# Fused attention and two feed-forward layers: heads, loads and gate sums of the opening rearranged

## The chip, the cores and the metric

One core of a Trainium2 chip runs the whole program. TensorE (PE) multiplies matrices, VectorE (DVE), ScalarE (ACT) and GpSimd (POOL) work on elements, SyncE (SP) issues most transfers, and ACT's queue can issue some. The metric is the device time of one execution in microseconds (us), as the median of several runs.

## What is computed

The reference, cut to its core: causal attention with a decay by the cumulative sum of logged gates, over 4 x 8 heads of 576 rows and 64 columns, and then two feed-forward layers on 2304 rows.

```python
scores = scale * np.matmul(q, k.transpose(0, 1, 3, 2))        # 4 x 8 heads, 576 x 64
cum = np.cumsum(np.log(np.clip(f, 0.0001, 1.0)), axis=-1)
decay = cum[:, :, :, None] - cum[:, :, None, :]
scores = np.where(causal, -1000000000.0, scores + decay)
attn = softmax(scores)
x = (attn @ v), laid out as 2304 x 512
h = x @ w_in;  x = np.maximum(0.01 * h, h) @ w_out            # 512 -> 2048 -> 512
h = x @ w_in2; out = (h * sigmoid(h)) @ w_out2
```

The term `cum[:, :, :, None]` is the same for all keys of a row, and a softmax over the keys does not change by it.

## The kernel before

**Tiling.** Each sequence of 576 rows is cut into a first half of 256 rows (two blocks of queries) and a second of 320 (three). A unit of work is a head of one half: heads 0 to 7 are the eight heads of the first half of sequence 0, heads 8 to 15 those of its second half, and so on to 63. The rows that attention gives go to tiles named ring, in two parts (a rounded one and the rest). When the first 256 rows are complete (all of heads 0 to 7), `hidden` starts: products named hps of ring tiles with weights w, in steps of two weights of 128 columns; `summed` adds their outcome into acc. The words of the weights are loaded (`first_weights`, issued in `fetch`), and converted by ACT and DVE into two parts (`conv_in`, `conv_out`: one ACT step at L1478, DVE steps at L1479, L1480 and L1482, a rounding by ACT and a difference by DVE at L307).

**A head.** `score` issues for each block of queries a product (sps) and, on DVE, a minimum with the mask (L668), then on ACT an exponential (L711); the sums of the shares, their reciprocal (`shares`) and the scaling (L719 on DVE or L721 on ACT) follow. `transp` transposes the shares on PE (tps, L770), they are copied to pf, and `weigh_pair` multiplies two heads with their values (av, L840) and writes the ring. `attention` (L918) sets the order: the product of head n, then a wait for the transposes ("tail") of head n-1, then the transposes of head n are started and the product of head n+1 follows.

**Gates.** `gates` loads fs (L405 for 512 rows, L403 for the last 64), has it clamped (`clamp`, L331, by GpSimd), takes logs on ACT, loads the table for the exponential ("warm", L417) and sums along the rows by products with a triangle, cps (L429). Heads 0 and 1 (`n < DIRECT`) add the gates in their own product from fs and the triangle (L681). The other heads have two more rows under the 64 of q and k: beside the queries the negated sum and ones, beside the keys ones and the sum. For heads 2 to 7 `first_rows` copies them from cps into cfr (L485 on DVE, L486 on ACT) and SP moves them into the tiles of q and k (L143 in the profile, two transfers for each pair of heads). From head 8 on they come from memory: `plain_rows` writes cum_p (three rows), `split_rows` writes cum_d (six rows, split into a rounded part and the rest), and each head loads its rows from these.

**Order.** A planner (`Plan`) runs at build time: every step is a generator that asks for an engine with a cost and a rank, the lowest rank that is ready goes first, and what the planner picks is the order in which each engine's instructions stand in the program. Its costs set the order alone and no time on the chip. Where PE has nothing ready before the first hps, it gets a filler, a product into fps that nothing reads (`fillers`, L392 and L395); fillers end when the planner has issued the first step of hps. Conversions of weights have rank 1, the work of heads rank 0. Word loads wait for cf (the gate rows of `first_rows` made), those from the third on for "rows" (these rows landed). SP issues one transfer after the other; a wait ahead of it holds all behind it.

Of the kernel before, what the change touches and what calls it, by code (L numbers as in the profile page):

```python
# [19 lines left out]
STG_BUFS = 3  # L20
# [14 lines left out]
DIRECT = 2  # L35
EARLY = 2
FAVOR = 0.3
LAT = 0.11
PE_LAT = 0.4
# [29 lines left out]
class Plan:  # L69
# [8 lines left out]
    def __init__(self):  # L78
        self.now, self.count = 0.0, 0
        self.events, self.ready, self.free = [], {}, {}  # L80
        self.seen, self.waiting = {}, {}
        self.taken, self.given, self.queue = {}, {}, {}
        self.dma_free = 0.0
        self.filler = {}
# [46 lines left out]
    def issue(self, eng):  # L131
# [11 lines left out]
        fn()  # L143
        end = self.free[eng] = self.now + cost
# [95 lines left out]
def fused_kernel(ctx, tc, qt, kt, va, vb, ft, w1, wi2, wo2, out):  # L240
# [26 lines left out]
    cum_d = dram.tile([H * B, 6, S], F32, name="cum_d")  # L267
    cum_p = dram.tile([H * B, 3, S], F32, name="cum_p")
# [44 lines left out]
    def build_consts():  # L313
# [14 lines left out]
        def clamp(k):  # L328
            n, sl = opened["parts"][k]
            yield wait(("fs", k))  # L330
            yield op("pool", 0.35, lambda: nc.gpsimd.tensor_scalar(  # L331
# [5 lines left out]
        def fills():  # L337
# [9 lines left out]
            for r in range(2):  # L347
                yield zero(0.25, cum_rows[0][r][:, 1 - r], 1.0)
            signal("ones")

        def selects():
# [6 lines left out]
            yield from clamp(0)  # L358
            yield from clamp(1)
# [11 lines left out]
        yield par(fills(), selects())  # L371

    cum_rows = {}

    def gates(cp):
# [5 lines left out]
        cp3 = cp.tile([H * B, 3, S], F32, name="cp3")  # L381
        cr = cp.tile([H * B, 6, S], F32R, name="cr")
        warm = cp.tile([1, 1], F32, name="warm")
        z = cp.tile([128, 256], F32R, name="z")
        opened.update(tri=tri, fs=fs, parts=parts, ones=(cp3[:, 1, :], f32(cr[:, 2:4, :])))
# [14 lines left out]
        def logs(k):  # L400
            n, sl = parts[k]
            if k:
                yield dma(8e3, lambda: nc.sync.dma_start(out=fs[0:n, nfull, :], in_=ft[nfull * 128:S, :]), -1)  # L403
            else:
# [12 lines left out]
                    op("act", 1.4, lambda: nc.scalar.activation(warm, fs[0:1, 0, 0:1], ACTF.Exp), 0)))  # L417
        pss = []
        banks = []
        for i, (t0, tn) in enumerate(HALF):  # L420
# [12 lines left out]
            for piece in ([todo] if i == 0 else [[c] for c in todo]):  # L433
                yield op("pe", sum(pe_cost(tn - 128 * c + t0, 4) for c in piece),
                         lambda: [sums(c) for c in piece], 1 if i else -1)
            pss.append(ps)
            if i == 0:
                cf = cum_rows[0]
                p.start(first_rows(ps, cf))
        signal("cum")  # L440

        def plain_rows():
            yield wait("rows_set")
            for i, ((t0, tn), ps) in enumerate(zip(HALF, pss)):
                w = slice(t0, t0 + tn)
                if i == 0:
                    yield act(tn, lambda: nc.scalar.copy(cp3[:, 2, w], ps), 0)
                    yield wait(("cf", 0), ("cf", 1))
                else:
                    yield dve(tn, lambda: nc.vector.tensor_scalar(  # L450
                        cp3[:, 2, w], ps, cp3[:, 2, t0 - 1:t0], None, op0=ALU.add), 0)
                give(("av", "sp")[i], banks[i])
                yield dve(tn, lambda: nc.vector.tensor_scalar(
                    cp3[:, 0, w], cp3[:, 2, w], -1.0, None, op0=ALU.mult), 0, True)
            yield dma(221e3, lambda: nc.sync.dma_start(out=cum_p, in_=cp3), 0)
            signal("cum_p")

        def split_rows():
            c, hi, lo = cp3[:, 0], cr[:, 0], cr[:, 1]
            yield act(S, lambda: nc.scalar.copy(hi, c))  # L460
            yield dve(S, lambda: nc.vector.tensor_tensor(lo, c, f32(hi), op=ALU.subtract))
            for dst, src in ((cr[:, 4], hi), (cr[:, 5], lo)):
                yield act(S, lambda: nc.scalar.mul(dst, f32(src), -1.0))
            yield dma(442e3, lambda: nc.sync.dma_start(out=cum_d, in_=f32(cr)))
# [7 lines left out]
    def first_rows(ps, cf):  # L472

        def rows(r, step):
            yield wait("ones")
            yield step
            signal(("cf", r))
            yield par(*[seq(
                dma(8e3, partial(nc.sync.dma_start, out=first[i][64 + r:65 + r], in_=cf[r][2 * i:2 * i + 2]), i - H),
                signals(("row", r, i)),  # L480
            ) for i in range(DIRECT // 2, H // 2)])
            give("stg", cum_rows[1][r])

        yield par(
            rows(0, dve(256, lambda: nc.vector.tensor_scalar(cf[0][:, 0], ps[0:H], -1.0, None, op0=ALU.mult), 0)),  # L485
            rows(1, act(256, lambda: nc.scalar.copy(cf[1][:, 1], ps[0:H]), 0)),  # L486
        )
# [31 lines left out]
    def load_first():  # L519
# [3 lines left out]
        def group(i):  # L523

            t = first[i] = slot(i, [66, 2, 2, tn], F32, "qk0")
            def move(r, src):
                dst, src_ = t[0:64, :, r], src[0, 2 * i:2 * i + 2, 0:64, 0:tn].rearrange("h d s -> d h s")
                if i == 0 and r:
                    yield op("act", 0.6, lambda: nc.scalar.dma_start(out=dst, in_=src_), 0, 2.0)
                else:  # L530
                    yield dma(131e3, lambda: nc.sync.dma_start(out=dst, in_=src_), 0 if i else -2)

            if i > 1:
                yield wait(("cf", 0), ("cf", 1))
            yield par(move(0, qt), move(1, kt))
            if 2 * i >= DIRECT:
                yield wait(("row", 0, i), ("row", 1, i))
# [18 lines left out]
    def load_head(n):  # L556
# [30 lines left out]
        if plain(n):  # L587
            k2 = hd.tile([66, ke], F32, tag="m1", name="k2")
            s1 = hd.tile([66, tn], F32, tag="s1", name="s1")
            heads[n].update(s1=s1, m1=k2)  # L590
            if e == 0:
# [4 lines left out]
                seq(wait("cum_p"), dma(4e3, lambda: nc.sync.dma_start(out=k2[64:66], in_=cum_p[g, 1:3, 0:ke]), 0)),  # L596
                seq(wait("cum_p"), dma(4e3, lambda: nc.sync.dma_start(out=s1[64:66], in_=cum_p[g, 0:2, t0:ke]), 0)),
# [7 lines left out]
        m2 = hd.tile([68, ke], F32R, tag="m2", name="m2")  # L605
        s1 = hd.tile([128, tn], F32R, tag="s1", name="s1")
        s2 = hd.tile([68, tn], F32R, tag="s2", name="s2")
# [15 lines left out]
        def rows():  # L623
            yield wait("cum_d")
            yield dma(4e3, lambda: nc.sync.dma_start(out=f32(s2[64:68]), in_=cum_d[g, 0:4, t0:ke]), 0)
            yield dma(4e3, lambda: nc.sync.dma_start(out=f32(m2[64:68]), in_=cum_d[g, 2:6, 0:ke]), 0)
# [9 lines left out]
    def loads():  # L636
# [5 lines left out]
        yield wait(("cf", 0), ("cf", 1))  # L642
# [1139 lines left out]
```

## Time and profile before

| what | us |
|---|---|
| median of 3 runs (994.35 to 1001.07) | 994.56 |
| profiled execution, time | 996.5 |
| its span, first to last instruction | 994.7 |
| PE busy in the span | 988.4 |
| DVE busy | 770.7 |
| ACT busy | 637.3 |

The mean granted clock of PE is 0.999 of full. A busy PE is not PE at its peak: matmuls are pipelined and their ends are modelled, and the fillers count as busy. The opening is the first 48 us, in which the first eight heads run, the first weights are converted and PE gets fillers.

### The profile page before, as it was taken

How to read it: one execution, taken by the hardware profiler on the slowest of the kernel's cores; microseconds unless marked ns; L12 is line 12 of the kernel's file. 1: busy time of each engine (PE TensorE's matmuls, PEld its weight loads, DVE VectorE, ACT ScalarE, POOL GpSimd, SP SyncE). 2: the span in 40 equal slices, each digit the busy share in tenths (PEclk: the TensorE clock that was granted, in tenths of full speed). 3: DMA queues.
4: the chain of work that ended last, by engine and by line, in shares of the span. 5: the costliest groups of instructions: out<-in, count | busy, mean ns of one | idle time of the engine just before them, and what ended most of it. 6: DMA issues, size and time to landing. Idle time of an engine off the chain costs nothing.

```text
span 994.7 us, 21101 instructions
## 1 busy us (share of the span) xinstructions
PE 988.4 (99%) x7911; PEld 951.3 (96%) x7911; DVE 770.7 (77%) x1843; ACT 637.3 (64%) x1389; POOL 107.9 (11%) x137
## 2 busy tenths in 40 slices
PE   9999999999999999999999999999999999999998
PEld 7777779999999999999999999999999999999998
DVE  6998968878888787887767799566762389988884
ACT  6866567667787777887664667565654576444442
POOL 2000003122222222342111010000000000000000
PEclk9999999999999999999999999999999999999999
DMA  6943433221242222332302686568985586445442
GB/s 202 309 127 118 146 112 108 65 85 42 74 128 72 85 60 60 93 114 82 105 29 101 222 302 219 186 227 287 333 299 198 164 281 191 149 134 163 128 128 64
DMA packets 98238, 148.99 MB, mean 150 GB/s; under 512 B 8324, under 2 KB 69404, under 8 KB 96056
## 3 DMA queue, kind: packets, MB, share of 16 engines
q1 hardware_dynamic: 97992, 147.51, 46.0%
q8 instruction: 62, 1.02, 0.4%
q14 instruction: 40, 0.33, 0.1%
q10 hardware_dynamic: 144, 0.13, 0.1%
HBM read 99.21 MB, written 43.66 MB: 144 GB/s over the span
## 4 chain that ended last, share of the span: by engine, by line
PE 95%; DMA 3%; SPq 1%; DVE 0%; ACT 0%; issue 0%; DVEq 0%
PE hps L970 21%; PE acc L1049 19%; PE m L1264 18%; PE m L1435 18%; PE sps L688 6%; PE tps L770 5%; PE av L881 4%; PE acc L1043 2%; PE av L840 1%; DMA wsd<-in_w_dram 1%; DMA wsg<-in_w_dram 1%; DMA s<-cum_p 1%; DMA wsr<-in_w_dram 1%; PE fps L392 0%; SPq L1520 0%
## 5 line engine op out<-in xcount | busy, mean ns | idle before, releaser
L970 PE MATMUL hps<-ring,w 128*128 128x256 f32 x1728 | 259.3, 287 | 0.0
L970 PEld LDWEIGHTS hps<-ring,w 128*128 128x128 f32 x1728 | 228.5, 191 | 4.5 <-issue 2.9
L1049 PE MATMUL acc<-g,dec 128*128 128x256 f32 x1344 | 199.3, 285 | 0.0
L1264 PE MATMUL m<-xc,w 128*128 128x256 f32 x1536 | 185.4, 282 | 0.0
L1264 PEld LDWEIGHTS m<-xc,w 128*128 128x128 f32 x1536 | 184.3, 191 | 0.0
L1435 PE MATMUL m<-w,gc 128*128 128x256 f32 x1512 | 182.3, 283 | 0.0
L1435 PEld LDWEIGHTS m<-w,gc 128*128 128x128 f32 x1512 | 181.6, 191 | 0.6
L1049 PEld LDWEIGHTS acc<-g,dec 128*128 128x128 f32 x1344 | 177.3, 191 | 0.5
L299 ACT CAST gc<-g 128x512 fp32r<-128x512 f32 (+1 forms) x144 | 79.0, 567 | 82.8 <-DVE g L1097 35.6
L711 ACT ACTIVATE sc<-sc,st 128x576 f32<-128x576 f32 (+4 forms) x160 | 93.0, 582 | 51.8 <-DVE st L668 50.8
L299 ACT CAST dec<-wo 128x512 fp32r<-128x512 f32 x112 | 69.5, 620 | 46.4 <-PE acc L1049 46.0
L307 DVE TENSOR_TENSOR gc<-g,gc 128x512 fp32r<-128x512 f32 (+1 forms) x144 | 87.2, 620 | 8.2 <-ACT gc L299 6.9
L668 DVE CUSTOM_DVE_ANT_0 sc<-sps,zmask 128x288 f32<-128x288 f32 (+4 forms) x160 | 72.1, 452 | 17.8 <-PE sps L688 12.0
L307 DVE TENSOR_TENSOR dec<-wo,dec 128x512 fp32r<-128x512 f32 x89 | 62.9, 707 | 25.1 <-ACT dec L299 24.6
L770 PE MATMUL tps<-ident,sc 66*107 66x66 f32 (+3 forms) x480 | 66.6, 268 | 0.5 <-DVE sc L719 0.4
L788 DVE TENSOR_TENSOR pl<-tps,pt 107x320 fp32r<-107x320 f32 (+2 forms) x114 | 54.4, 509 | 14.9 <-ACT pt L787 14.3
L1097 DVE TENSOR_TENSOR g<-g 128x256 f32<-128x256 f32 x144 | 58.8, 420 | 8.4 <-DMA g<-g_d 7.5
L688 PE MATMUL sps<-m,s 68*128 68x288 f32 (+9 forms) x264 | 59.9, 308 | 0.0
L770 PEld LDWEIGHTS tps<-ident,sc 66*107 66x107 f32 (+3 forms) x480 | 54.4, 151 | 4.3 <-issue 1.8
L787 ACT CAST pt<-tps 107x320 fp32r<-107x320 f32 (+2 forms) x114 | 45.9, 447 | 16.8 <-PE tps L770 16.3
L307 DVE TENSOR_TENSOR g<-hps,g 128x512 fp32r<-128x512 f32 x65 | 44.6, 686 | 15.6 <-ACT g L299 14.8
L1000 ACT ACTIVATE hps<-hps 128x512 f32<-128x512 f32 x65 | 37.9, 583 | 23.0 <-PE hps L970 22.2
(140 smaller groups left out, 1389.5 us busy)
## 6 DMA issues: line engine op xcount, KB each, us to landing
g_d<-z SPq DMA_DIRECT2D x16, 1024.0 KB
g<-g_d SPq DMA_DIRECT2D x32, 512.0 KB
w_d<-f SPq DMA_DIRECT2D x16, 896.0 KB
ws<-w_d SPq DMA_DIRECT2D x56, 256.0 KB
wst<-in_wi_dram SPq DMA_DIRECT2D x16, 512.0 KB
wst<-in_wo_dram SPq DMA_DIRECT2D x16, 512.0 KB
qk<-in_kt_dram SPq DMA_DIRECT2D x24, 288.0 KB
wss<-in_w_dram SPq DMA_DIRECT2D x10, 512.0 KB
```

Of the source, the lines that this page charges most:

```text
L299: ("act", act_cost(n, base), lambda: nc.scalar.copy(dst, src), 0.0),
L307: ("dve", dve_cost(n), lambda: nc.vector.tensor_tensor(dst, a, b, op=ALU.subtract), 0.0),
L668: yield dve(w, lambda: nc.vector.tensor_tensor_reduce(out=sc[0:qn, k0:k0 + w], in0=ps[0:qn], in1=zmask[0:qn, z0:z0 + w], scale=-0.125, sca ...
L688: nc.tensor.matmul(ps[0:qn], ht[x][:, qs], ht[y][:, k0:k0 + w], start=r == 0, stop=r == len(ops) - 1)
L711: yield act(kn, lambda: nc.scalar.activation(sc[0:qn, 0:kn], sc[0:qn, 0:kn], ACTF.Exp, scale=-1.0, bias=st[0:qn, 2 * i + a:2 * i + a + 1], ...
L770: nc.tensor.transpose(ps[0:k1 - k0, o:o + qn], ht["p"][i][0:qn, k0:k1], ident[0:qn, 0:qn])
L788: yield op("dve", dve_cost(width), lambda: nc.vector.tensor_tensor(pts[1][0:kw], ps[0:kw], f32(pt[0:kw]), op=ALU.subtract), 0, PE_LAT)
L970: nc.tensor.matmul(hp_t[:, part], w[:, wi, c * 128:(c + 1) * 128], x[xi][:, c, :], start=(part == 0 and c == 0 and r == 0), stop=(c == KC ...
L1049: nc.tensor.matmul(o, w[:, wi, c * 128:(c + 1) * 128], g[:, gi, part * T:(part + 1) * T], start=(start and r == 0 and c % 2 == 0), stop=(s ...
L1097: ("dve", dve_cost(n), lambda: nc.vector.tensor_tensor(dst, a, b, op=op_), 0.0),
L1264: nc.tensor.matmul(dst[:, a], w[:, wi, c * 128:(c + 1) * 128], x[:, xi, c], start=start and a == 0 and c == 0 and r == 0, stop=stop and c ...
L1435: nc.tensor.matmul(banks[b][:, e], t[:, gi, a * 128:(a + 1) * 128], w[:, wi], start=begin and a == 0 and r == 0, stop=jp == NP // 2 - 1 an ...
```

## The change

Three heads are under way in place of two while the first eight run: the wait ahead of the next head is for the transposes of all heads up to n-2 (`AHEAD`). The loads of q and k for heads 4 to 7 no longer wait for the gate rows; their key loads, as that of heads 0 and 1 already, go by ACT's queue, those of heads 4 to 7 behind the load of the Exp table. Ranks of the first loads change. The clamp goes from GpSimd to DVE. The queries' gate row is dropped everywhere: products have 65 (or 64 + 66) rows, `first_rows` makes one row with ACT alone and moves three rows in place of six, cum_p has two rows and cum_d four, and the negations on DVE and ACT go. The sums cps of the first half get rank 0.5 in place of -1, the cum_p transfer -1 in place of 0. A transpose asks for its PSUM bank after its SBUF tiles. The planner starts its time at 0.85 us, doubles PE's costs ahead of 6.9 us and adds 0.13 us to every hand-over but SP's ahead of 45 us. No line of the diff changes how many word loads may be under way.

```diff
+AHEAD = 2
+OPEN = 0.85
+COLD = 6.9
+TIGHT = 45.0
+HOP = 0.13
-        self.now, self.count = 0.0, 0
+        self.now, self.count = OPEN, 0
         fn()
+        if eng == "pe" and self.now < COLD:
+            cost *= 2
+        if eng != "sp" and self.now < TIGHT:
+            lat = (LAT if lat is None else lat) + HOP
...
-    cum_d = dram.tile([H * B, 6, S], F32, name="cum_d")
-    cum_p = dram.tile([H * B, 3, S], F32, name="cum_p")
+    cum_d = dram.tile([H * B, 4, S], F32, name="cum_d")
+    cum_p = dram.tile([H * B, 2, S], F32, name="cum_p")
...
-            yield op("pool", 0.35, lambda: nc.gpsimd.tensor_scalar(
+            yield op("dve", 0.2, lambda: nc.vector.tensor_scalar(
                 fs[0:n, sl], fs[0:n, sl], 0.0001, 1.0, op0=ALU.max, op1=ALU.min), 0)
...
-                yield dma(8e3, lambda: nc.sync.dma_start(out=fs[0:n, nfull, :], in_=ft[nfull * 128:S, :]), -1)
+                yield dma(8e3, lambda: nc.sync.dma_start(out=fs[0:n, nfull, :], in_=ft[nfull * 128:S, :]), -2.5)
...
-                    op("act", 1.4, lambda: nc.scalar.activation(warm, fs[0:1, 0, 0:1], ACTF.Exp), 0)))
+                    op("act", 1.4, lambda: nc.scalar.activation(warm, fs[0:1, 0, 0:1], ACTF.Exp), -1), signals("warm")))
...
-                         lambda: [sums(c) for c in piece], 1 if i else -1)
+                         lambda: [sums(c) for c in piece], 1 if i else 0.5)
...
-                yield dve(tn, lambda: nc.vector.tensor_scalar(
-                    cp3[:, 0, w], cp3[:, 2, w], -1.0, None, op0=ALU.mult), 0, True)
-            yield dma(221e3, lambda: nc.sync.dma_start(out=cum_p, in_=cp3), 0)
+            yield dma(147e3, lambda: nc.sync.dma_start(out=cum_p, in_=cp3), -1)
...
-            for dst, src in ((cr[:, 4], hi), (cr[:, 5], lo)):
-                yield act(S, lambda: nc.scalar.mul(dst, f32(src), -1.0))
-            yield dma(442e3, lambda: nc.sync.dma_start(out=cum_d, in_=f32(cr)))
+            yield dma(295e3, lambda: nc.sync.dma_start(out=cum_d, in_=f32(cr)))
...
-        yield par(
-            rows(0, dve(256, lambda: nc.vector.tensor_scalar(cf[0][:, 0], ps[0:H], -1.0, None, op0=ALU.mult), 0)),
-            rows(1, act(256, lambda: nc.scalar.copy(cf[1][:, 1], ps[0:H]), 0)),
-        )
+        yield wait("ones")
+        yield act(256, lambda: nc.scalar.copy(cf[:, 1], ps[0:H]), 0)
+        signal("cf")
+        yield par(*[seq(
+            dma(8e3, partial(nc.sync.dma_start, out=first[i][64:65], in_=cf[2 * i:2 * i + 2]), i - H),
+            signals(("row", i)),
+        ) for i in range(DIRECT // 2, H // 2)])
...
-                if i == 0 and r:
-                    yield op("act", 0.6, lambda: nc.scalar.dma_start(out=dst, in_=src_), 0, 2.0)
+                if r and i != 1:
+                    if i:
+                        yield wait("warm")
+                    yield op("act", 0.6, lambda: nc.scalar.dma_start(out=dst, in_=src_), 0 if i else -2, 2.0)
                 else:
-                    yield dma(131e3, lambda: nc.sync.dma_start(out=dst, in_=src_), 0 if i else -2)
-
-            if i > 1:
-                yield wait(("cf", 0), ("cf", 1))
+                    yield dma(131e3, lambda: nc.sync.dma_start(out=dst, in_=src_), -2 if i else -2.6)
...
-            i_sp = yield take("sp", 3)
-            ps = ps_at.tile([128, width], F32, tag="sp", name="tps")
...
+        for w in work:
+            w[4] = yield take("sp", 3)
+            w[3] = ps_at.tile([128, w[2]], F32, tag="sp", name="tps")
...
-            if prev is not None:
-                yield wait(("tail", prev))
+            back = AHEAD if n < H - 1 else 1
+            yield wait(*[("tail", m) for m in range(max(0, n - H), n - back + 1)])
...
-        yield wait(("cf", 0), ("cf", 1), "v0_sent")
+        yield wait("cf", "v0_sent")
```

## Rows read from the trace of the kernel before

**Rows 1.** The page's first part: busy us, share of the span, instructions.

```profile
PE 988.4 (99%) x7911; PEld 951.3 (96%) x7911; DVE 770.7 (77%) x1843; ACT 637.3 (64%) x1389; POOL 107.9 (11%) x137
```

**Rows 2.** Tile fps: count, ns min/median/max of one, first and last start in us.

```profile
L395 PE MATMUL fps<-zmask x112: 272/275/377, 12.3 to 42.1; 128*128 128x128 f32 x112
L392 PE MATMUL fps<-z x15: 415/415/583, 1.3 to 4.4; 128*128 128x256 f32 x15
```

**Rows 3.** Stretches: length; busy PE, PEld, DVE, ACT, POOL; PE clock; DMA share; GB/s.

```profile
6.00:12.00 6.00, 6.00 (x26) 3.53 (x25) 2.35 (x12) 3.98 (x11) 2.05 (x5) 1.00 0.67 209
12.00:18.00 6.00, 6.00 (x49) 5.06 (x48) 5.31 (x24) 4.33 (x13) 0.00 (x0) 1.00 0.65 201
18.00:42.00 24.00, 24.00 (x178) 19.13 (x175) 22.05 (x73) 20.48 (x57) 0.00 (x0) 1.00 0.95 301
42.00:48.00 6.00, 5.48 (x41) 4.87 (x40) 4.85 (x14) 4.69 (x10) 0.00 (x0) 1.00 0.97 281
48.00:100.00 52.00, 51.95 (x321) 39.28 (x321) 47.26 (x122) 34.29 (x77) 0.00 (x0) 1.00 0.41 129
```

**Rows 4.** PE in order of time: start us, us, line, operation, names, count.

```profile
4.76 1.49 PE L429 MATMUL cps<-tri,fs 128*32 128x256 f32 x4
6.18 0.72 PE L679 MATMUL sps<-qk 64*128 64x128 f32 x2
...
12.93 0.49 PE L770 MATMUL tps<-ident,sc 128*128 128x128 f32 x3
...
25.63 2.84 PE L395 MATMUL fps<-zmask 128*128 128x128 f32 x24
...
33.59 0.49 PE L770 MATMUL tps<-ident,sc 128*128 128x128 f32 x3
...
39.64 0.96 PE L970 MATMUL hps<-ring,w 128*128 128x256 f32 x6
...
979.50 11.20 PE L1435 MATMUL m<-w,gc 128*128 128x256 f32 x92
```

**Rows 5.** DVE by line, 6 to 42 us: busy us, mean ns | idle before.

```profile
L668 DVE CUSTOM_DVE_ANT_0 sc<-sps,zmask 128x128 f32<-128x128 f32 (+4 forms) x21 | 8.3, 396 | 4.5 <-PE sps L681 3.6 <-PE sps L688 0.8
...
L307 DVE TENSOR_TENSOR w<-ct,w 128x512 fp32r<-128x512 f32 x4 | 2.7, 687 | 0.0
L1480 DVE SCALAR_TENSOR_TENSOR ct<-cy,ct 128x512 int32<-128x512 int32 x4 | 2.7, 684 | 0.0
L1482 DVE SCALAR_TENSOR_TENSOR ct<-wsr,ct 128x512 int32<-128x512 int32 x3 | 2.0, 678 | 0.0
...
L453 DVE TENSOR_SCALAR cp<-cp 32x256 f32<-32x256 f32 (+1 forms) x2 | 0.6, 284 | 0.0
...
L485 DVE TENSOR_SCALAR cfr<-cps 8x256 f32<-8x256 f32 x1 | 0.4, 413 | 3.7 <-PE cps L429 3.7
```

**Rows 6.** PE by line, 0 to 12.2 us: the products of heads 0 and 1.

```profile
L681 PE MATMUL sps<-tri,fs 128*128 128x128 f32 (+1 forms) x12 | 2.8, 343 | 0.0
L679 PE MATMUL sps<-qk 64*128 64x128 f32 (+1 forms) x8 | 2.6, 410 | 0.0
```

**Rows 7.** In order of time: the clamp, and the fourth weight's last step.

```profile
2.97 0.64 POOL L331 TENSOR_SCALAR fs<-fs 128x128 f32<-128x128 f32 x1 [0.53 <-DMA fs<-in_ft_dram]
...
40.40 0.69 DVE L307 TENSOR_TENSOR w<-ct,w 128x512 fp32r<-128x512 f32 x1
```

**Rows 8.** Issues of transfers in order of time, by ACT's and SP's queue.

```profile
0.81 0.71 ACTq L529 DMA_DIRECT2D qk<-in_kt_dram  x1
...
6.73 1.47 SPq L143 DMA_DIRECT2D qk<-cfr  x2
8.24 0.86 SPq L1520 DMA_DIRECT2D wsr<-in_w_dram  x2
...
11.58 0.67 SPq L531 DMA_DIRECT2D qk<-in_qt_dram  x1
...
19.20 0.42 SPq L1520 DMA_DIRECT2D wsr<-in_w_dram  x1
```

## What I predict, blind

> **What bounds the kernel now.** I read the page's first part first: TensorE (PE) is busy for 99% of the span [rows 1]. That number hides the opening, because the kernel itself keeps PE busy there with products that nothing reads. So the second view is that of one tile, fps, the target of these fillers: 15 of them before 4.4 us and 112 between 12.3 and 42.1 us [rows 2]. A run of 24 takes 2.84 us [rows 4], 0.118 us each, so the 112 cost 13.2 us; the first 15 cost 3.6 us. Behind 42.1 us there are none.
>
> The third view is the table of stretches [rows 3]. From 48 to 100 us PE is uncovered for 0.05 us, so from there on nothing is won by starting single pieces sooner: what the opening saves shifts the rest forward as a block. The same table says what paces the opening. VectorE (DVE) works 5.31 of 6 us and then 22.05 of 24 from 12 to 42 us, which is 27.36 of 30, or 91%; ScalarE (ACT) has 24.81 of 30. From 6 to 12 us DVE has only 2.35 of 6.
>
> The fourth view is the order of time on PE [rows 4]. The transposes of heads 0 and 7 start at 12.93 and 33.59 us, so the eight heads of the first block pass at 20.66/7 = 2.95 us each, and the first hidden product of the network (hps) starts at 39.64 us, 6.05 us behind the last of them. Fillers run until then. So the questions are by how much hps comes forward, and whether PE is fed from there.
>
> **The change, part by part.** *The first head.* Today the gate sums (cps) go ahead of head 0's product: they start at 4.76 us, and the product (sps) starts at 6.18 [rows 4]. DVE waits 3.7 us until cps ends, and then 3.6 us in all for the four products of heads 0 and 1 [rows 5]. With rank 0.5 in place of -1 the sums go behind products that are ready, so head 0 starts up to 6.18 - 4.76 = 1.42 us sooner. The clamp, 0.64 us on GpSimd [rows 7], moves to DVE, which waits then; the trace has no clamp by DVE. Its nearest tensor_scalar, two of 0.28 us at the mean [rows 5], would save 0.36 us; at the price of GpSimd it saves nothing. The bounds of both edits together are 0 and 1.42 + 0.36 = 1.8 us. Against the upper end stands that head 0 moves into the slow stretch: the first 15 products of 256 columns are 3.6/15 = 0.24 us apart [rows 2], those at the end 11.20/92 = 0.122 [rows 4], though the table shows a granted clock of 1.00, that is 2.4 GHz, throughout. For it stands that the third head also falls into the 3.65 us that DVE has idle from 6 to 12 us. I take 1.8.
>
> What the moved sums delay: the products of heads 0 and 1 keep PE 2.6 + 2.8 = 5.4 us [rows 6], 2.7 us a head, so the gate row cf comes up to 2.7 us later, and with it the rows of heads 2 to 7 and all word loads, which wait on cf. The first words go out at 8.24 us now [rows 8], then by 10.9. I cost this at nothing, because the heads' work on DVE covers it; without that cover it costs up to 2.7 us.
>
> *Work that is gone.* DVE loses the negated gate row, 0.41 us, and two negations of the plain rows, 0.57 us together [rows 5]: 0.98 us, all at the place where it sets the pace. I count 1.0; nothing if the holes stay empty. A fill of ones goes too, where DVE waits anyway: nothing. ACT loses two negations and gains two load issues of 0.71 us each [rows 8]; even without the loss, 1.42 us lie in the 5.2 that ACT has idle in those 30: nothing, and 1.42 without that cover. One row less in a product changes no column count: no PE time. cum_d and cum_p lose three rows of 32 x 576 values of 4 bytes, 0.22 MB; at 301 GB/s [rows 3] this is 0.7 us of transfer, hidden by DVE's pace, and worth 0.7 us where transfers bound.
>
> *Queues.* SP issues without a pause from 6.73 us on: gate rows at 1.47/2 = 0.74 us each, loads at 0.67; the third word goes at 19.20 [rows 8]. Three gate rows go, 2.2 us. The four loads of heads 4 to 7 leave this stretch, 4 x 0.67 = 2.7 us: two go to ACT behind its Exp table, two to an earlier place on SP. So SP gains 4.9 us and gives up to 2.7 back by the late cf; later words come 2.2 to 4.9 us sooner. The transfers are 0.65 to 0.67 busy from 6 to 18 us and 0.95 from 18 to 42 [rows 3], so there is room ahead of 18 us. Worth nothing by itself, but it lets the words keep step with a shift of some 4 us.
>
> A rule speaks against these edits: by the Trainium skill (DMA: Bandwidth & Descriptors, Issuing engines are not separate DMA queues) issuing from several engines saves only the issue time, which it calls small beside the transfer. The trace agrees only in part: an issue takes 0.67 to 0.74 us on a queue without a pause [rows 8]. By the rule the early loads would bring nothing, as in the second rival; by the rows they move words by 2.2 us or more.
>
> *The third head.* Now the product of head n+1 waits for the transposes of head n-1, then for those of n-2. This can only fill DVE's holes from 12 to 42 us, 2.64 us. I take half, 1.3; bounds 0 and 2.6. The later request for a bank in the transposes and the planner's hops of 0.13 us change the order alone, and no row shows them; beyond 48 us the nearest is the 0.05 us that PE loses, so I take nothing, with the 0.5 us that PE loses from 42 to 48 [rows 3] as the other bound, a loss or a gain.
>
> *Sum.* 1.8 + 1.0 + 1.3 = 4.1 us. The profiled execution has a span of 994.7 us and a time of 996.5, which is 1.9 above the runs' median of 994.56. So the span would be 990.6, the profiled time 992.4, and the median 990.4 us, which I predict.
>
> **The rivals.** *Heads quicker than DVE's share allows.* With three heads under way the eight may pass at DVE's and ACT's bare work, and the 6.05 us behind the last may shrink; hps would come 6.5 to 10 us sooner. For it: 13.2 us of fillers are there to take. Against it: DVE has 3.65 + 2.64 = 6.3 us idle from 6 to 42 us, and with the 0.98 that goes, 7.3 us is the most unless conversions are left for after hps. Time 984.6 to 988.
>
> *The transfers set the pace.* They are 0.95 to 0.97 busy from 18 to 48 us [rows 3]. If so, heads finish sooner and hps waits for weights; the 0.7 us of bytes and up to 1.4 of the earlier start are left: 992.5 to 993.9. Against it: DVE, at 91%, hardly waits on a load there.
>
> *Slower: heads starve the weights.* Heads have rank 0 on DVE and ACT, conversions rank 1. Three of a conversion's four DVE steps take 0.69 + 0.68 + 0.68 = 2.05 us [rows 5]. The second hidden step needs the fourth weight, ready now at 41.09 us [rows 7], 1.45 us behind the first hps. If the third head and late words push conversions back by two, PE meets a hole without fillers, which end with the first step: 4.1 us later weights, less the 1.45, 2.7 us lost, 997.3; with the words' 2.7 on top, 1000. It decides where the fourth weight is ready later than 42.5 us. For it: DVE's 91%. Against it: the work ahead of that weight is the same sum, less 0.98.
>
> *It does not do what it says.* The words are called unlimited, but nothing in the diff alters how many are loaded, and the key loads of heads 4 to 7 wait for the Exp table and are not at once. If heads keep today's pace for that, the first head's gain alone is left, at most 1.8 us: 992.7 to 994.5.
>
> **How the numbers follow.** Forecast, 988 to 992.5: 0.50. Transfers bound, 0.12, and no third head in effect, 0.08, both 992.5 to 994.6. Quicker heads, below 988: 0.17, of which 0.05 below 984.6. Slower than 994.6: 0.13, of which 0.03 above 1004.5, where more than the priced delays would have to meet. About 1% (9.9 us) is what a measurement of this kernel can tell from no change, so faster has 0.05, same 0.92, slower 0.03. The range leaves out the ends of the two outer cases, 985.5 to 997.0; the forecast's own is 988 to 992.5.
>
> **What the profile would show.** Right: head 0's sps near 4.8 us, transposes of heads 0 and 7 near 11 and 29.5, hps near 35.5; some 4 us fewer fillers, about 78 records; DVE at 95% or more from 12 to 36 us; PE still covered from 48 us on. Wrong: as many fillers as now; PE waiting for w or a load between 36 and 48 us; first words behind 11 us; a span that moves by another amount than hps.

## The result, and the profile after

The changed kernel takes 1004.48 us (median of 5 runs, 1002.41 to 1007.24), the kernel before 994.93 beside it (994.35 to 1001.07): a ratio of 1.0084, 95% interval 1.0057 to 1.0111. It is slower by 8 to 10 us: the interval lies above 1, though mostly within the 1% that the prediction took for no change. The time is outside the range of 985.5 to 997.0, and the forecast of 990.4 had the sign wrong. The profiled execution took 1007.24 us, with a span of 1005.5 against 994.7.

The page's first part of the changed kernel, to hold against [rows 1]:

```profile
PE 994.8 (99%) x7883; PEld 953.4 (95%) x7883; DVE 769.4 (77%) x1839; ACT 637.6 (63%) x1388; POOL 108.9 (11%) x136
```

PE's share is again 99%, and says as little as before. The stretches, against [rows 3]; columns as there:

```profile
6.00:12.00 6.00, 6.00 (x16) 2.84 (x14) 0.73 (x4) 1.86 (x7) 0.35 (x1) 1.00 0.81 224
12.00:18.00 6.00, 6.00 (x19) 3.73 (x19) 1.26 (x7) 1.74 (x6) 0.00 (x0) 1.00 0.61 176
18.00:42.00 24.00, 24.00 (x154) 18.45 (x152) 20.05 (x77) 17.48 (x51) 0.00 (x0) 1.00 0.83 268
```

From 12 to 18 us PE is covered throughout and yet gets through 19 products where it did 49, and DVE works 1.26 of 6 us instead of 5.31. The granted clock is shown as 1.00, but that is no reading of these stretches: the first record of the clock in this trace starts at 23.53 us (in the kernel before at 6.70), and ahead of it the view prints 1.00. PE in order of time, against [rows 4], says what happened:

```profile
4.75 0.79 PE L675 MATMUL sps<-qk 64*128 64x128 f32 x2
...
6.20 1.49 PE L436 MATMUL cps<-tri,fs 128*32 128x256 f32 x4
...
18.30 0.85 PE L767 MATMUL tps<-ident,sc 128*128 128x128 f32 x3
...
18.94 1.06 PE L684 MATMUL sps<-qk 65*128 65x256 f32 x2
...
20.64 1.49 PE L402 MATMUL fps<-zmask 128*128 128x128 f32 x6
...
25.03 0.60 PE L684 MATMUL sps<-qk 65*128 65x256 f32 x2
...
32.58 1.95 PE L402 MATMUL fps<-zmask 128*128 128x128 f32 x16
...
38.45 0.55 PE L767 MATMUL tps<-ident,sc 128*128 128x128 f32 x3
...
44.31 0.96 PE L965 MATMUL hps<-ring,w 128*128 128x256 f32 x6
```

The same two products take 1.06 us at 18.94 and 0.60 at 25.03. Until about 23.5 us every product goes at half the later pace; before, the pair of products at 6.18 us is the last that is slow. The transposes of head 0 come at 18.30 us instead of 12.93, and hps at 44.31 instead of 39.64. Here PE is the limit of the opening, which no step of the prediction had.

That is half of the loss. For the rest I laid both traces over each other by PE's own work: fillers left out, each product counted by its columns at full pace (957.9 us in all, the same in both), and the time read at which PE has done so much of it. Kernels of the experiments below stand beside it; a minus is a lead over the kernel before.

| work done, us | 25 | 90 | 100 | 200 | 300 | 400 | 600 | 800 | end |
|---|---|---|---|---|---|---|---|---|---|
| before, at us | 45.83 | 112.83 | 123.91 | 226.59 | 328.44 | 430.15 | 630.98 | 831.31 | 989.46 |
| changed | +4.90 | +4.54 | +5.79 | +5.02 | +7.11 | +9.05 | +10.83 | +10.72 | +10.76 |
| e1 | -0.17 | -0.78 | -0.62 | -1.13 | +0.95 | +2.88 | +4.69 | +4.53 | +4.44 |
| e4 | -4.53 | -3.47 | -4.23 | -4.82 | -2.71 | -0.76 | +1.05 | +2.22 | +3.32 |
| e5 | -2.24 | -1.88 | -1.88 | -1.92 | -1.91 | -1.90 | -1.90 | -0.99 | -0.04 |
| e6 | -4.25 | -3.68 | -3.68 | -3.71 | -3.70 | -3.71 | -3.72 | -3.20 | -2.39 |
| e7 | -0.38 | -1.30 | -1.30 | -1.32 | -0.38 | +0.54 | +1.29 | +2.87 | +2.60 |
| e13 | -1.48 | -1.04 | +0.21 | -0.55 | +1.51 | +3.48 | +5.33 | +5.02 | +4.74 |
| e10 | -0.47 | -0.46 | -0.46 | -0.46 | -0.45 | -0.45 | -0.45 | -0.52 | -0.58 |
| e14 | -4.47 | -3.77 | -3.77 | -3.79 | -3.79 | -3.76 | -3.78 | -3.14 | -2.67 |

The table compares single executions. That of the kernel before, at 996.5 us, lies 1.0 to 1.9 us above the medians of 994.56 to 995.49 that this kernel has in all, so by medians the leads are smaller by that; that of the changed kernel is the slowest of its five.

The changed kernel has lost 4.9 us by 50 us, loses 1.25 at about 123 us, gains 0.8 back by 230, and loses 5.8 between 230 and 642 us, where it computes the same as before. PE's waits from 200 to 640 us (total us, times, longest); the kernel before has none in this stretch:

```profile
PE hps L965 <- DVE g L317: 1.5, 1, 1.5
PE av L878 <- DVE xf L891: 0.5, 1, 0.5
PE tps L767 <- DVE sc L715: 0.4, 1, 0.4
PE sps L684 <- DVE pl L785: 0.2, 1, 0.2
PE av L878 <- DVE pl L785: 0.2, 1, 0.2
PE av L878 <- DVE ring L310: 0.2, 1, 0.2
```

Each is a short wait for a piece of DVE's work. Ahead of the longest, ACT and DVE each do a step of a weight w directly before theirs of the g that PE waits for; how much of the 1.5 us this costs, and what stands ahead in the other waits, isn't shown:

```profile
598.68 0.61 ACT L1677 CAST w<-ws 128x512 fp32r<-128x512 f32 x1
599.18 0.58 ACT L309 CAST g<-hps 128x512 fp32r<-128x512 f32 x1
...
599.32 0.69 DVE L317 TENSOR_TENSOR w<-ws,w 128x512 fp32r<-128x512 f32 x1 [0.21 <-ACT w L1677]
599.92 0.68 DVE L317 TENSOR_TENSOR g<-hps,g 128x512 fp32r<-128x512 f32 x1
...
600.75 0.95 PE L965 MATMUL hps<-ring,w 128*128 128x256 f32 x6 [1.48 <-DVE g L317]
```

The same view of waits from 48 to 200 us has one row, a word of the second weights:

```profile
PE acc L1038 <- DVE wo L1477: 2.0, 1, 2.0
```

### The profile page after: what moved, and what is told of

Read it like the earlier page. It is cut to its first block, busy times and chain, and to the rows that moved or that the text cites. A ratio compares the mean times of both kernels' runs of the same rounds, so it can differ in the third digit from the quotient of the medians.

```text
span 1005.5 us, 21027 instructions
## 1 busy us (share of the span) xinstructions
PE 994.8 (99%) x7883; PEld 953.4 (95%) x7883; DVE 769.4 (77%) x1839; ACT 637.6 (63%) x1388; POOL 108.9 (11%) x136
## 4 chain that ended last, share of the span: by engine, by line
PE 91%; DVE 4%; ACT 2%; DMA 1%; issue 1%; POOL 0%; DVEq 0%; POOLq 0%; ACTq 0%
PE hps L965 19%; PE m L1259 18%; PE acc L1044 17%; PE m L1430 15%; PE sps L684 6%; PE tps L767 5%; PE av L878 4%; PE acc L1038 2%; PE av L837 2%; PE fps L402 1%; DVE gc L317 1%; DMA g<-g_d 1%; DVE w L317 1%; DMA ws<-w_d 0%; PE sps L677 0%
## 5 line engine op out<-in xcount | busy, mean ns | idle before, releaser
L664 DVE CUSTOM_DVE_ANT_0 sc<-sps,zmask 128x288 f32<-128x288 f32 (+4 forms) x160 | 71.7, 449 | 23.5 <-PE sps L684 12.1
L317 DVE TENSOR_TENSOR dec<-wo,dec 128x512 fp32r<-128x512 f32 x86 | 60.1, 699 | 28.4 <-ACT dec L309 27.9
L316 POOL TENSOR_TENSOR dec<-wo,dec 128x512 fp32r<-128x512 f32 x26 | 35.6, 1368 | 243.5 <-ACT dec L309 231.1
L684 PE MATMUL sps<-m,s 66*128 66x288 f32 (+9 forms) x264 | 60.2, 309 | 0.2 <-DVE pl L785 0.2
```

The costliest lines, as they stand in the source:

```text
L317: ("dve", dve_cost(n), lambda: nc.vector.tensor_tensor(dst, a, b, op=ALU.subtract), 0.0),
L664: yield dve(w, lambda: nc.vector.tensor_tensor_reduce(out=sc[0:qn, k0:k0 + w], in0=ps[0:qn], in1=zmask[0:qn, z0:z0 + w], scale=-0.125, sca ...
L684: nc.tensor.matmul(ps[0:qn], ht[x][:, qs], ht[y][:, k0:k0 + w], start=r == 0, stop=r == len(ops) - 1)
```

## The experiments

Three causes were put against each other. *Order*: the planner plans the whole program anew, so an edit of the opening changes the order of steps hundreds of us later, and the new order stalls. *Pace*: PE's first products stay at half pace longer. *Feed*: the heads or the transfers of the opening starve what comes behind. All times are medians with the range of the runs, and each ratio is to the kernel before, run beside it; none of these kernels changes what is computed.

**One part undone at a time.** e1 puts the sums first again, e2 takes the third head away, e3 does the late sums alone in the kernel before, e4 takes away the planner's opening.

```diff
# e1, in the changed kernel
-                         lambda: [sums(c) for c in piece], 1 if i else 0.5)
+                         lambda: [sums(c) for c in piece], 1 if i else -1)
# e2, in the changed kernel
-AHEAD = 2
+AHEAD = 1
# e3, in the kernel before
-                         lambda: [sums(c) for c in piece], 1 if i else -1)
+                         lambda: [sums(c) for c in piece], 1 if i else 0.5)
# e4, in the changed kernel
-OPEN = 0.85
-COLD = 6.9
-TIGHT = 45.0
+OPEN = 0.0
+COLD = 0.0
+TIGHT = 0.0
```

> The changed kernel with one edit: the gate sums of the first half get rank -1 again, so they go ahead of head 0's product. Theory A (clock): in the changed kernel PE's products go at half the pace until about 23 us (same shape 0.21 to 0.25 us apart, later 0.11), in the kernel before until about 6.7 us, and the sums' new place among the first products is what keeps PE at the lower level. Then here products are at the full pace from about 7 us, the transposes of head 0 start before 13.5 us (18.3 in the changed kernel), the first hps before 39 us (44.3), and the time is 992 to 998 us. Theory B (the third head and the new order of loads crowd DVE and PE): nothing of that moves, time 1002 to 1007 us. Theory C (the planner's new costs pick a worse order behind the opening): the opening is better, but the 5 us lost between 240 and 640 us stay, time 997 to 1000 us.

> The changed kernel with one edit: AHEAD = 1, so only two of the first eight heads are under way. Theory A (clock): the order of the first products is the same as in the changed kernel, so PE stays at half the pace until 15 us or later, first hps at 43 to 47 us, time 1001 to 1008 us. Theory B (the third head crowds): first hps near 39.6 us as in the kernel before, time 993 to 997 us. Theory C: no statement on the opening, the 5 us between 240 and 640 us may stay or go, as the order there is picked anew.

> The kernel before with one edit: the gate sums of the first half get rank 0.5 in place of -1, so head 0's first product goes ahead of them. Theory A (clock): the edit alone keeps PE at half the pace beyond 10 us, the transposes of head 0 start later than 15 us (12.9), the first hps later than 42 us (39.6), time 998 to 1006 us. Theory B and C: PE is at the full pace from about 7 us, head 0 starts 1 us sooner, first hps at 38.5 to 40 us, time 993 to 996 us.

> The changed kernel with the planner's start, doubled costs and hops set to zero (OPEN, COLD, TIGHT = 0), which also brings the sums ahead of head 0's product and takes one filler out at the start. Theory A (clock): full pace from about 7 us and first hps before 40 us unless the missing filler leaves a hole that keeps PE at half the pace; time 992 to 999 us. Theory B: as the changed kernel, 1002 to 1007 us. Theory C (the planner's new costs): the losses behind 240 us go too, below 2 us in all, time 990 to 996 us.

Measured: e1 1000.9 us (1000.69 to 1001.97, ratio 1.0064), e2 1002.86 (1002.52 to 1007.75, 1.0093), e3 1002.59 (1001.36 to 1004.19, 1.008), e4 998.74 (997.98 to 1006.01, ratio 1.004, interval 1.0011 to 1.0069). All four had PE at full pace by 7 us in their profiles, and all four are slower than the kernel before. So the late pace isn't the whole loss, and no single part carries it. Each theory misses somewhere: A, since e2 and e3 have the late sums and full pace early; B, since e2, without the third head, is no quicker; C, since e4 was to come out at 996 us or less. e3 is telling: one rank changed, an opening that is 2.3 us ahead (hps at 37.30 us), and 7.5 us lost, a part of it to a fall of the clock at 50 us (last section). e4's opening is the one that was forecast; PE in order of time:

```profile
4.55 1.38 PE L436 MATMUL cps<-tri,fs 128*32 128x256 f32 x4
...
29.86 0.49 PE L767 MATMUL tps<-ident,sc 128*128 128x128 f32 x3
...
35.00 0.96 PE L965 MATMUL hps<-ring,w 128*128 128x256 f32 x6
```

Its lead is 4.5 us at 41 us and still 4.8 at 222 us, and yet it ends 3.3 behind. Its stretches from 200 to 640 us (columns as in [rows 3]), and below them those of the kernel before:

```profile
200.00:400.00 200.00, 198.39 (x1631) 196.03 (x1629) 162.28 (x448) 151.00 (x375) 51.35 (x65) 1.00 0.27 76
400.00:640.00 240.00, 238.42 (x1973) 237.25 (x1972) 187.08 (x404) 157.23 (x331) 41.49 (x43) 1.00 0.43 140
...
200.00:400.00 200.00, 200.00 (x1657) 199.15 (x1656) 163.00 (x447) 153.08 (x379) 47.20 (x61) 1.00 0.27 76
400.00:640.00 240.00, 240.00 (x1992) 239.46 (x1992) 191.11 (x421) 160.73 (x344) 41.46 (x46) 1.00 0.43 145
```

PE is uncovered for 1.61 + 1.58 us there, against 0 in both stretches before, and PE's waits are the six of the changed kernel, within 0.1 us. Starving by the opening doesn't fit: the opening is ahead, and the first 200 us lose nothing.

**The old order behind the opening.** e5 is the changed kernel, e6 is e4, e9 is e1, each with the planner held to the kernel before: every step that its plan issues behind 60 us (by the planner's own time) keeps the engine and the place that it has there.

```diff
-            eng, cost, fn, _ = min(choices, key=end)
+            eng, cost, fn, _ = min([c for c in choices if c[0] == self.place.get(key, c[0])], key=end)
...
     def issue(self, eng):
-        queue = self.ready.get(eng)
...
+        ready, order = self.ready.get(eng, []), self.order.get(eng)
+        queue = [x for x in ready if x[-1] not in self.place or (order and x[-1] == order[-1])]
```

e7 goes the other way: the kernel before with one number of the planner changed by 2%; in its trace PE's products come in the order of the kernel before until 277 us. e8 is the changed kernel once more.

```diff
# e7, in the kernel before
-LAT = 0.11
+LAT = 0.112
```

> The changed kernel, whole, but the planner takes every step that the kernel before issued behind 60 us of the planner's time in the order, and on the engine, in which the kernel before issued it; only the opening is picked anew. Theory C (what the change loses behind the opening is lost by the order that the planner picks there anew, and by nothing that the change does): the stalls of PE between 200 and 640 us, 3.2 us uncovered in the changed kernel, fall below 0.6 us, and the time is that of the kernel before plus the opening's own shift, 991 to 998 us. Theory D (the change's own parts, the 65 rows, the later bank request, the smaller sums, cost time behind the opening): the stalls stay, 1000 to 1004 us.

> The changed kernel with OPEN, COLD and TIGHT at zero, where the opening is 4.5 us ahead of the kernel before until 200 us and all of it is lost by the end, and the old order behind 60 us of the planner's time. Theory C: the 4.5 us stay to the end, 989.5 to 992 us, faster than both kernels. Theory D: 997 to 1000 us as without the old order.

> The kernel before with one number of the planner changed, LAT 0.112 in place of 0.11: no work, no wait and no load differs, PE's instructions stand in the same order up to the 648th row of 2286, and behind it the order is picked anew. Theory C: the same opening (first hps at 39.6 us within 0.3), and 2 to 8 us lost behind 200 us: 997 to 1003 us. Theory D: no loss, 994 to 996 us.

> The changed kernel once more, for a second profile and its time beside the others. If the half pace of PE until 23 us in its first profile is a matter of chance in each execution, this profile may show the full pace from about 6.5 us on, with the first hps 3 to 6 us sooner than 44.3 and a time of about 1002 us; if it belongs to the kernel's order, products are at half the pace until 15 us or later here too, and the time is 1004 to 1007 us.

> The changed kernel with the gate sums ahead of head 0's product (rank -1) and the old order behind 60 us of the planner's time. Theory E (two separate losses: the new order behind the opening, some 5 to 6 us, and a pace of PE that in many executions rises late because of what PE does behind its first fillers, 0 to 7 us): both are gone, every run within 1.5 us of the others, median 993.5 to 995.5 us, where the same kernel with the sums late had 996.5 to 1003.8. Rival F (the spread of that kernel's runs has nothing to do with the first products): runs spread over 4 us or more here too, median 997 to 1001 us.

Measured: e6 994.18 us (993.83 to 994.53, ratio 0.9988, interval 0.9973 to 1.0003) where e4 had 998.74: the order alone is worth 4.6 us. It was expected at 989.5 to 992; the lead is kept to 630 us and not to the end (the table). e7 999.32 (998.89 to 1000.6, 1.004, interval 1.0026 to 1.0055): 4.2 us lost by a number that no instruction carries out, with an opening that is 0.4 us ahead. From 112 to 226 us e7 is 1.3 us ahead of the kernel before, with the same order of PE's products and a clock whose first record starts at 5.83 us in place of 6.70; so a lead of that size in a single profile need not come from an edit. PE's waits of e7, 200 to 980 us, the first three; they are of the same sort:

```profile
PE av L881 <- DVE xf L894: 0.5, 1, 0.5
PE m L1264 <- ACT w L1682: 0.5, 1, 0.5
PE m L1264 <- DVE w L307: 0.3, 1, 0.3
```

e8 came out at 1007.01 (1003.37 to 1009.47), with half pace until 20.8 us. e5 came out at 1000.68 (996.46 to 1003.81), far wider than e6. Its profiled execution was one of the quickest, and had full pace early:

```profile
4.75 0.79 PE L928 MATMUL sps<-qk 64*128 64x128 f32 x2
5.48 0.57 PE L930 MATMUL sps<-tri,fs 128*128 128x128 f32 x2
5.98 0.84 PE L689 MATMUL cps<-tri,fs 128*32 128x256 f32 x4
...
12.62 0.49 PE L1020 MATMUL tps<-ident,sc 128*128 128x128 f32 x3
...
37.18 0.96 PE L1218 MATMUL hps<-ring,w 128*128 128x256 f32 x6
```

The four sums that took 1.49 us in the changed kernel take 0.84 here, and with the same plan of the opening hps starts at 37.18 us instead of 44.31. So the late pace costs the opening up to 7.1 us, and it comes in some executions and not in others. I took it for a matter of the sums' place, since all profiles with the sums first had had full pace early. e9 ended that: with the sums first it has 996.59 us (995.4 to 1002.27, ratio 1.0014; a tenth run, of 2273 us, is left out, and nothing recorded says why it took so long), but its profiled execution, of 1002.27 us, had half pace until 20.8 us and hps at 46.28.

**Products against the late pace.** e10 is e5 with 14 more filler products of 256 columns ahead of head 0's first product; e13 is the same with the changed kernel's own order held behind 60 us in place of that of the kernel before. e11 is e4 with three numbers of the planner searched for an earlier planned end, e12 is e6 once more, and e14 is e6 with 8 more fillers.

```diff
# e10 and e13 with 14, e14 with 8
             p.issue("pe")
+            yield wait("tri", ("logs", 0))
+            yield op("pe", 0.12 * 14, lambda: [
+                nc.tensor.matmul(fps, z[:, 0:128], z, start=True, stop=True) for _ in range(14)], -9)
             yield wait("zmask", ("scored", 0, 0))
# e11, on top of e4
-FAVOR = 0.3
-LAT = 0.11
-PE_LAT = 0.4
+FAVOR = 0.2681
+LAT = 0.1197
+PE_LAT = 0.3341
```

> The changed kernel with the old order behind 60 us and 14 more fillers of 256 columns on PE between the first 15 and head 0's product; the sums stay late. This delays head 0 by 1.7 to 3.3 us and keeps PE on full products until about 8 us. Theory E: PE reaches the full pace by 8 us in the profile, all runs within 2 us of each other, median 996 to 999 us in spite of the delay (1000.7 without the fillers). Rival F: runs spread over 4 us or more, median 1002 to 1004 us, which is 1000.7 and the delay.

> The changed kernel with OPEN, COLD and TIGHT at zero and other planner numbers (LAT 0.1197, FAVOR 0.2681, PE_LAT 0.3341), the choice whose plan ends first of 40, 2.8 us ahead of the plan with the given numbers. If the planner's own end is a measure of the order behind the opening, 995 to 997.5 us; if the stalls behind 200 us come from what the planner doesn't see, 997 to 1001 us.

> The version with the changed opening, the planner's numbers at zero and the old order once more, for a closer interval against the kernel before. Expected 0.5 to 2.5 us below the kernel before (its profile showed 2.3 us), runs within 1 us of each other, since the sums are first and PE is at the full pace from about 6 us.

> The changed kernel with 14 more fillers ahead of head 0's product, as in e10, but behind 60 us of the planner's time every step in the order that the changed kernel itself has. So it differs from e10 in that order alone, and from the changed kernel in the fillers. If the changed kernel's loss is two losses, a late pace of PE and its order, this one has the order's loss without the late pace: full pace by 8 us, all runs within 2 us of each other, median 1000.5 to 1003 us, 4.5 to 6.5 us above e10. If the late pace is all of the loss, 995.5 to 997.5 us as e10; if fillers don't cure the late pace in this order, runs spread over 4 us and a median of 1004 us.

> The changed kernel with OPEN, COLD and TIGHT at zero, the old order behind 60 us, and 8 fillers in place of 14 ahead of head 0's product. If 8 are enough for the full pace, the opening keeps 2 to 3 of its 3.7 us lead, every run lies within 1.5 us and the median is 993.3 to 995 us; if not, two or more of ten runs lie 5 us or more above the others, as five of twelve did without these fillers.

Measured: e10 996.16 us (995.42 to 996.8, ratio 1.0004), where e5 reached 1003.81: the spread is gone, and the fillers give up 2.2 us of hps for it (39.42 against 37.18). e13 1002.75 (1001.22 to 1003.29, ratio 1.0052, interval 1.0027 to 1.0078). These two differ in the order behind 60 us alone, 6.6 us (the kernel before beside them has 995.49 and 995.33). Their stretches, e13 first:

```profile
48.00:200.00 152.00, 149.14 (x1031) 124.82 (x1030) 126.09 (x348) 104.27 (x253) 12.56 (x15) 1.00 0.37 110
200.00:400.00 200.00, 198.41 (x1631) 196.04 (x1629) 163.18 (x440) 152.11 (x375) 49.89 (x64) 1.00 0.27 74
400.00:640.00 240.00, 238.43 (x1972) 237.27 (x1972) 189.69 (x418) 157.96 (x337) 42.47 (x45) 1.00 0.42 137
```

and e10:

```profile
48.00:200.00 152.00, 150.54 (x1042) 126.06 (x1041) 127.07 (x346) 101.89 (x247) 14.75 (x16) 1.00 0.36 109
200.00:400.00 200.00, 200.00 (x1657) 199.17 (x1656) 163.40 (x446) 153.56 (x380) 47.28 (x62) 1.00 0.27 75
400.00:640.00 240.00, 240.00 (x1992) 239.46 (x1992) 190.89 (x421) 160.59 (x343) 40.77 (x46) 1.00 0.44 144
```

PE goes uncovered for 1.40 us more from 48 to 200 us, 1.59 from 200 to 400 and 1.57 from 400 to 640, 4.6 of the 5.3 us by which the profiled spans differ (999.5 and 994.2). The rest of the 6.6 us by medians goes with the clock: e13's profiled execution is the quickest of its ten, and its mean granted clock is 0.999, as in one more of them (1001.38 us), while the other eight have 0.997 or 0.998 and 1001.96 to 1003.29 us, some 1.5 us more. All runs of e10 have 0.999 or 1.000. So in most runs the new order seems to bring a fall of the clock too; the traces of e8 and e3 show where one lies (last section).

e11 has 993.73 us (993.18 to 998.83, ratio 0.9984, interval 0.9964 to 1.0005), below the 995 to 997.5 expected and 5 us below e4, from which three numbers of the planner part it; its profiled execution is the one of 998.83, with half pace until 20.8 us, and PE is uncovered for 0.6 us from 200 to 640 us where e4 has 3.2. So here the plan that ends first by the planner's own time has an order that hardly stalls. e12 has 995.05 (994.08 to 1000.95, ratio 1.0008), where it was expected below the kernel before and within 1 us, with five of its 12 runs from 1000.59 to 1000.95 and the rest from 994.08 to 995.46: the kernel of e6, which showed none such in 10. e14 has 994.31 us (993.62 to 994.86), ratio 0.9968, interval 0.9944 to 0.9991, against 995.33: the one version whose interval against the kernel before lies below 1. By medians it gains 1.0 us; the rest of the ratio is that the kernel before had five late executions in the 19 beside it and e14 none. PE in order of time in e14:

```profile
13.23 0.49 PE L1023 MATMUL tps<-ident,sc 128*128 128x128 f32 x3
...
29.31 0.49 PE L1023 MATMUL tps<-ident,sc 128*128 128x128 f32 x3
...
34.77 0.95 PE L1221 MATMUL hps<-ring,w 128*128 128x256 f32 x6
```

It keeps 3.7 to 3.8 us of lead from 112 to 790 us and gives back 1.0 between there and 870 us, in short waits of the last layer for its rounded input (waits of PE's weight loads, then of PE, 640 to 980 us):

```profile
PEld m L1686 <- DVE gc L570: 1.0, 2, 0.5
PEld m L1686 <- ACT gc L562: 0.5, 2, 0.3
...
PE m L1686 <- DVE gc L570: 0.6, 2, 0.3
```

## Why the prediction was wrong

**The step that failed** is "what the opening saves shifts the rest forward as a block", with its companion, the hops and the bank request "change the order alone … so I take nothing", 0.5 us as the other bound. PE's 0.05 us uncovered from 48 to 100 us [rows 3] was read as slack that belongs to the program. It belongs to one order of it, and the planner writes a new one for each edit: 6.6 us between e13 and e10, 4.6 between e4 and e6, 4.2 for a planner's number changed by 2% (e7). With the old order held, the block did shift as I said: e5, e6, e10 and e14 keep their lead to within 0.1 us from 112 to 630 us (the table). Yet the block doesn't reach the end: behind that, mostly between 790 and 870 us, in the last layer, e5 loses all of its 1.9 us, e6 1.3 of 3.7 and e14 1.1 of 3.8. So even with the order held, less than the opening's gain is left.

**The slow stretch** was seen and not priced. I noted the first products at 0.24 us, and still took the upper end of 1.8 us for a head that moves into them. The sum had no term for a stretch that ends later: 44.31 - 37.18 = 7.1 us of hps between two executions of the same opening. By medians it is less, 1004.48 - 1002.75 = 1.7 us against e13, and 1007.01 - 1002.75 = 4.3 with the changed kernel's repeat, e8, in part because e13's fillers delay its hps (38.41 against 37.18); in which of these runs the pace came late isn't recorded. The granted clock of 1.00 that the prediction set beside the 0.24 us was no reading either: ahead of 6.70 us the trace has no record of it.

**The opening's own sum** of 4.1 us was too high for the change as it is, whose hps at full pace comes 2.5 us sooner (e5), and near for the change without the planner's opening (4.6 us, e4); its terms were off. With full pace early, hps starts at 39.64 us before, 37.18 with the change (e5), 37.30 with the late sums alone (e3), 43.20 without the third head (e2), 40.31 with the sums first (e1), 35.00 with the sums first and no planned opening (e4).

- *The first head*, 1.8 us taken: sps did start at 4.75 us, the 1.4 us forecast, and the clamp takes 0.23 us on DVE for 0.64 on GpSimd. At full pace the term was too small: the late sums alone bring hps forward by 39.64 - 37.30 = 2.3 us in the kernel before (e3), and by 40.31 - 37.18 = 3.1 us within the changed kernel. But the best openings don't need it: in e4 and e14 the transposes of head 0 come later (14.26 and 13.23 us) than before.
- *The third head*, 1.3 us taken, 2.6 as bound: 43.20 - 37.18 = 6.0 us within the changed kernel. In e14 a head passes in (29.31 - 13.23)/7 = 2.30 us, against 2.95. The bound by DVE's idle time was too low, because it took all of DVE's work up to 42 us as ahead of hps; DVE works 27.0 of the 30 us from 12 to 42 in e14, as before, with hps 4.9 us sooner.
- *The planner's opening* (OPEN, COLD, TIGHT), nothing taken: 40.31 - 35.00 = 5.3 us lost, e1 against e4. Only the third head gives more than that.
- *Queues*: the first words go at 8.92 us, by the 10.9 allowed for; at full pace (e5) the third goes at 16.55 instead of 19.20, the 2.2 us and more of the sum.

**The rivals.** The slower one named 997 to 1000 us by heads that starve the weights. PE does wait 2.0 us for a converted word, but at 121.6 us and not between 36 and 48, and it is worth 1.25 us of the 10.8 in this execution, without the fall of the clock that e8 shows behind it. Transfers as the limit: from 18 to 42 us they are 0.98 busy in e14 and 0.95 before, so they may be what holds e14's opening; no run took bytes away, and it stays open. Of the signs listed, "a span that moves by another amount than hps" is the one that showed: +10.8 against +4.7 us.

**What stays open.** The runs show that the order costs the time and where PE then waits, not which of the planner's costs misleads it; e11's three numbers were changed together. Nor do they show why half pace lasts in one execution and not in the next.

## What to carry to other kernels

Where a planner or scheduler writes the order, an edit is a change of the whole order. Compare it once with the order behind the edit held as it was, and change a number that ought not to matter, to see how much the order alone moves the time; here that is 4 to 7 us of 995, more than the edit could give. Ask of each lead whether a later stretch keeps it. Read an engine's pace from the spacing of equal products, not from its busy share, and from several executions.

## What was not expected of the hardware

TensorE's first products go at half pace, 1.2 of 2.4 GHz, and the rise to full pace comes either at 4.3 to 6.7 us (12 of the 16 traces) or only at 20.8 to 23.5 (the changed kernel, e8, e9, e11), though PE is covered with products from 1.3 us on; the changed kernel and e5, whose openings are the same, show the one and the other. The stretches print a granted clock of 1.00 all through it, but no trace has a record of the clock ahead of the rise: its first record starts there, at 1.00. What shows the pace is the spacing, 0.25 against 0.12 us in the changed kernel: six fillers in 1.49 us at 20.64, sixteen in 1.95 at 32.58. Going by the times it differs between executions of one kernel too, by some 6 us: 994 and 1001 in e12. Runs of over 1000 us, which I take for these, were 12 of 94 of the kernel before. With 8 or 14 more products of 256 columns, one behind the other, ahead of the first head there was no such spread in 30 runs (e10, e13, e14), while every kernel without them that was run ten times or more showed it but e7 (and e6, whose repeat e12 showed it). That is a link, not a mechanism. The Trainium skill (TensorE: Matmul & The Clock Gate, Part 1: The HAM clock gate) says that the number of slow products at the start differs from run to run and that a model should not be fitted to one count. The runs agree: its size is 0.6% of the span, and as large as what this change was about.

A fall within the run showed as well, to half, with a record of the clock at 0.5. In e3 it comes at 50.1 us, 1.5 us behind a wait of 1.2 us that ends at 48.6. In e8 PE stood idle for 2 us at 121 us, and the granted clock was 0.57 of full over the 4 us behind it (two stretches of e8; the clock is the third column from the right):

```profile
120.00:123.00 3.00, 1.00 (x5) 0.84 (x5) 3.00 (x11) 1.38 (x5) 0.00 (x0) 1.00 0.18 50
123.00:127.00 4.00, 4.00 (x20) 3.45 (x18) 1.67 (x5) 1.96 (x4) 0.00 (x0) 0.57 0.92 300
```

The profiled execution of the changed kernel has the same wait of 2.0 us and no fall. The lag over the kernel before went from +3.05 to +5.95 us across it in e8, from +4.54 to +5.79 in the other: 1.65 us for the fall. By the mean granted clock, 0.997 or 0.998 in place of 0.999 or 1.000, most runs of these kernels seem to have such a fall: four of five of the changed kernel, three of four of its repeat e8, all four of e3 and eight of ten of e13. In the profiles of these kernels PE waits 1.2 to 2.0 us in one piece within the first 125 us. Of the other runs only one of e5 (0.994) has less than 0.999. Why the fall comes in one execution and not in the next isn't shown.
